# Running all sixteen retention pairs ahead of the gated unit's first sweep

## The chip, the core and the metric

The kernel is one program on one core of a Trainium2 chip. Five engines work side by side, each through its own queue in order: TensorE (PE in the profile, with its weight loads as PEld), VectorE (DVE), ScalarE (ACT), GpSimd (POOL) and the queue that issues most DMAs (SP). The metric is the device time of one execution in microseconds, and lower is better.

## The reference

Three layers follow each other on 2304 tokens (4 batches of 576) of 512 features:

```python
# 1. retention: 8 heads of 64, decay gamma per head
scores = scale * np.matmul(q, k.transpose(0, 1, 3, 2))
Dmat = np.where(rel >= 0, gamma[:, None, None] ** rel[None, :, :], 0.0)
x = np.matmul(scores * Dmat[None], v)            # -> (2304, 512)
# 2. gated unit behind an RMS norm, d_ff = 1536
xn = x / np.sqrt(np.mean(x * x, axis=-1, keepdims=True) + 1e-06) * rms_g
g = xn @ w_gate
x = g * (1.0 / (1.0 + np.exp(-g))) * (xn @ w_val) @ w_out
# 3. eight experts (512 -> 1024 -> 512), mixed by 8 rounds of Sinkhorn on exp(x @ w_gate)
for e in range(8):
    out += P[:, e:e + 1] * (np.maximum(x @ w1[e], 0.0) @ w2[e])
```

## The kernel before, in words

The program is recorded in the order in which the Python code runs, and each engine executes its instructions in that order; buffers of the tile pools and the waits on them are the only other ties. So the order of work around the change is an order written out by hand.

**Retention.** The 32 heads are worked in 16 pairs (4 batches of 4 pairs; pair `i` is written `sc_i`, `am_i`, `o_i`). A pair has 576 tokens in four blocks of 128 and a tail of 64. `scores(i)` makes k·q of each block and head on PE (tile `sc`, one PSUM buffer per head), and DVE masks it (`am`). `states(i)` makes k·v of each block (`u`), which ACT and DVE turn into running states (`block_states`). `outputs(i)` makes `o` and `ot` from `am`, the states and the tail `mt`; DVE writes them to `acc`, ACT squares them, POOL adds the squares of a batch's pairs. The pass of the loop for pair `i` issues `scores(i + 1)`, `states(i + 1)` and then `outputs(i)`. Since `sc` has one buffer per head, `scores(i + 1)` waits until DVE has made `am_i`.

**Norm.** `norm(b)` is a generator that the loop steps: sums over the features on PE (`ss`), the root on DVE and POOL, a spread over partitions by PE (`dg`, `rb`, `rbt`, then `y`), and for each 128 features a product on DVE (L404), a high part on ACT (`xhi`, L405) and a low part on DVE or POOL (`xlo`, L408 and L410).

**Gated unit.** `gated_block(s, t0, n, ...)` works `n` tokens with 256 of the 1536 inner features; a sweep `s` is all tokens, and there are six sweeps. A product of full precision is three fp32r matmuls (L174 to L176: high·high, high·low, low·high). A block has 48 of them for the gate and value (`gv`) and 24 for the way back (`x`). Behind each pair of `gv` DVE multiplies (L202), ACT takes the high part (`ghi`, L203) and DVE the low part (`glo`, L204), which the `x` matmuls read. In the first sweep ACT writes `x` to `acc` (L223), in the later ones DVE adds it (L225).

**Weights.** They arrive as 64-bit floats. `step_weights()` brings up to two pieces of 128x512 one step forward: a start (L122 on POOL, L123 and L124 on DVE), the sign step (L126 on DVE, L127 on ACT), a product (POOL), the high part into a slot (ACT) and the low part (L144 on DVE). There are seven slots (`wslots`, `NW = 7`); six pieces make a sweep.

**The first sweep in the retention.** Before, the first sweep runs over eight blocks of 288 tokens (`FIRST_BLOCKS`) as a stream (`dense`) out of which `fill()` takes a quarter of a block's `gv`, or half of its `x`, at a time, from pair 7 on, between `scores`/`states` and `outputs`. Earlier passes have `keep_busy(3)` at two places: three bf16 matmuls of 128x512 on a pad, whose result nobody reads. What is left of the stream runs behind the last pair, with the first block of the second sweep begun inside it (`second_sweep`). Sweeps 1 to 5 then run in a plain loop over five blocks of 512 or 384 tokens (`BLOCKS`).

Of the kernel before, what the change touches and what calls it, by code (L numbers as in the profile page):

```python
# [18 lines left out]
NP = H // 2  # L19
# [11 lines left out]
FIRST_BLOCKS = [(b * S + h * (S // 2), S // 2) for b in range(B) for h in range(2)]  # L31
# [6 lines left out]
N_DENSE = 15  # L38
# [12 lines left out]
def retention_glu_experts(ctx: ExitStack, tc: tile.TileContext, a, out):  # L51
# [43 lines left out]
    slots = [[(wslots[:, i, 0, :], wslots[:, i, 1, :]) for i in range(NW)], []]  # L95
    raw_slots = list(range(NRAW))
# [82 lines left out]
    def gated_block(s, t0, n, last, pmm, pac, hp, tp, together, w):  # L179
# [27 lines left out]
        for d0 in range(0, KD, together):  # L207
            ys = [(pac[0] if type(pac) is list else pac).tile([128, 512], F32, tag="ac", name=f"x{s}_{t0}_{d0 + d}") for d in range(together)]
# [24 lines left out]
    def in_turn(blocks):  # L233

        before = ()
        for ready, block in blocks:
            while not ready():
                yield
            next(block)
            yield  # L240
            for _ in before:
                yield
            for _ in range(2 * SWEEP - 1):
                next(block)
                yield
            before = block
        for _ in before:
            yield


    early = ExitStack()
    hp0 = early.enter_context(tc.tile_pool(name="hp0", bufs=SWEEP + 1))
    tp0 = early.enter_context(tc.tile_pool(name="tp0", bufs=2))
# [6 lines left out]
    pmm0 = early.enter_context(tc.tile_pool(name="pmm0", bufs=2, space=PSUM, side="right"))  # L260
    pac0 = early.enter_context(tc.tile_pool(name="pac0", bufs=2, space=PSUM, side="right"))
# [5 lines left out]
    mhalf = tabs.tile([128, NC + 1], F32, name="mhalf")  # L267
    block_states = [tabs.tile([128, NC, 2 * D], F32, name=f"block_states{i}") for i in range(2)]
# [3 lines left out]
    def load_pair(i):  # L272
        if i >= B * NP:
            return
        b, pr = divmod(i, NP)
        t = {}
        for n in ("kT", "qT", "ks", "vs"):
            t[n] = ld.tile([128, a[n].shape[-1]], F32, tag=n, name=f"{n}{i}", bufs=2 if n[0] == "k" else 3)
            nc.sync.dma_start(t[n], a[n][b, pr])
        loaded[i] = t  # L280
# [34 lines left out]
    def states(i):  # L315
# [12 lines left out]
        for h, hs in enumerate(heads):  # L328
            nc.scalar.mul(st[hs, :, hs], u[hs, :NC, :], g_step[hs, pr:pr + 1])
# [7 lines left out]
    def outputs(i):  # L337
# [4 lines left out]
        o = psa.tile([128, NC, C], F32, tag="o", name=f"o{i}")  # L342
        ot = pac0.tile([128, 512], F32, tag="ac", name=f"ot{i}")[:, :TAIL]
# [25 lines left out]
    normed = set()  # L369

    def norm(b):

        sq = squares.pop(b)
        ss = pac0.tile([128, 512], F32, tag="ac", name=f"ss{b}")[:, :NC + 1]
# [3 lines left out]
        v = sp.tile([128, NC + 1], F32, tag="rv", name=f"rv{b}")  # L378
        r = sp.tile([128, NC + 1], F32, tag="ry", name=f"ry{b}")
        t = sp.tile([128, NC + 1], F32, tag="rt", name=f"rt{b}")  # L380
# [8 lines left out]
        dg = sp.tile([128, (NC + 1) * C], F32, tag="dg", name=f"dg{b}", bufs=1)  # L389
# [23 lines left out]
    def first_group():  # L413
        for t0, n in FIRST_BLOCKS:
            block = gated_block(0, t0, n, t0 + n == NT, pmm0, pac0, hp0, tp0, 2, S // 2)
            yield (lambda b=t0 // S: b in normed), block

    dense = in_turn(first_group())

    norms = []  # L420

    def fill():
        next(dense, None)
        step_weights(load=False)

    def norm_step(n=1):
        for _ in range(n):
            if norms and next(norms[0], True):
                norms.pop(0)

    idle = pad[:, :128]
    idle_ps = pmm0.tile([128, 512], F32, tag="mm", name="idle_ps")
# [19 lines left out]
    load_pair(1)  # L452
# [6 lines left out]
    states(0)  # L459
    for i in range(B * NP):  # L460
        b, pr = divmod(i, NP)
        load_pair(i + 2)
# [5 lines left out]
        if i <= NP + 2:  # L468
            keep_busy(3)
        if i == NP + 1:  # L470
            norm_step()
        scores(i + 1)
        states(i + 1)
        if i <= NP + 1:
            keep_busy(3)
            outputs(i)
            for _ in range(3 if i < NP else 1):
                step_weights(load=False)
            if i >= NP:
# [35 lines left out]
    for _ in dense:  # L515
        pass
# [795 lines left out]
```

## Time and profile before

| | |
|---|---|
| time of three runs | 2068.27 us median (2065.36 to 2070.55) |
| profiled execution | 2068.53 us, span 2066.6 us from the first to the last instruction |
| mean granted TensorE clock | 0.992 of full speed |
| PE busy | 2035.1 us, 98% of the span |
| DVE busy | 1482.2 us, 72% |
| ACT, POOL busy | 862.9 us, 842.9 us |
| DMA | 211 GB/s in the mean |

The span is counted from the first instruction to the last; the execution's own time holds 1.9 us more. The granted clock is given as a share of 2.4 GHz, and 0.50 is the lower level of 1.2 GHz. A busy PE need not be a useful one: the filler matmuls count, and a matmul at the lower clock counts twice as long.

### The profile page before, as it was taken

How to read it: one execution, taken by the hardware profiler on the slowest of the kernel's cores; microseconds unless marked ns; L12 is line 12 of the kernel's file. 1: busy time of each engine (PE TensorE's matmuls, PEld its weight loads, DVE VectorE, ACT ScalarE, POOL GpSimd, SP SyncE). 2: the span in 40 equal slices, each digit the busy share in tenths (PEclk: the TensorE clock that was granted, in tenths of full speed). 3: DMA queues.
4: the chain of work that ended last, by engine and by line, in shares of the span. 5: the costliest groups of instructions: out<-in, count | busy, mean ns of one | idle time of the engine just before them, and what ended most of it. 6: DMA issues, size and time to landing. Idle time of an engine off the chain costs nothing.

```text
span 2066.6 us, 30376 instructions
## 1 busy us (share of the span) xinstructions
PE 2035.1 (98%) x11526; PEld 1883.8 (91%) x11526; DVE 1482.2 (72%) x2324; ACT 862.9 (42%) x1655; POOL 842.9 (41%) x746
## 2 busy tenths in 40 slices
PE   8999999999999999999999999999999999999998
PEld 5688788899788989999998999999999999999998
DVE  6764775653468887777776777777788677777777
ACT  3443331221254454444444544444445544444443
POOL 4411442310024454544561545444455454544443
PEclk8899999999999999999999999999999999999999
DMA  7420221100028888888878767676766676767673
GB/s 233 156 90 1 69 75 41 62 29 3 0 96 306 296 297 299 309 300 306 306 285 329 262 252 275 244 268 247 280 246 260 251 273 252 260 251 281 241 282 138
DMA packets 112690, 436.58 MB, mean 211 GB/s; under 512 B 12297, under 2 KB 30473, under 8 KB 96161
## 3 DMA queue, kind: packets, MB, share of 16 engines
q1 hardware_dynamic: 110048, 432.72, 57.4%
q8 instruction: 90, 1.47, 0.3%
q10 hardware_dynamic: 2496, 1.94, 0.3%
q14 instruction: 56, 0.45, 0.1%
HBM read 312.40 MB, written 122.21 MB: 210 GB/s over the span
## 4 chain that ended last, share of the span: by engine, by line
PE 89%; DVE 6%; ACT 2%; issue 1%; POOL 1%; DMA 1%; ACTq 0%; SPq 0%; DVEq 0%; POOLq 0%
PE pz L775 9%; PE py L775 9%; PE px L775 9%; PE qx L1006 6%; PE qy L1006 6%; PE qz L1006 6%; PE gv L174 5%; PE gv L175 4%; PE gv L176 4%; PE y L175 4%; PE y L176 4%; PE y L174 4%; PE qz L775 3%; PE x L174 2%; PE x L175 2%; PE x L176 2%
## 5 line engine op out<-in xcount | busy, mean ns | idle before, releaser
L1183 POOL TENSOR_TENSOR acc<-z,a_block 128x384 f32<-128x384 f32 x63 | 64.0, 1016 | 446.5 <-DVE z L1177 446.5
L775 PE MATMUL py<-sx,w1s 128*128 128x384 f32 x1152 | 233.0, 336 | 2.8 <-ACT py L1099 2.5
L775 PEld LDWEIGHTS py<-sx,w1s 128*128 128x128 f32 x1152 | 203.5, 188 | 7.2 <-ACT py L1099 4.3
L775 PE MATMUL px<-xhi,w1s 128*128 128x384 f32 x640 | 188.5, 335 | 0.0
L996 ACT CAST xhi<-acc 128x384 fp32r<-128x384 f32 x316 | 156.0, 514 | 69.6 <-POOL acc L1183 35.4
L1000 DVE TENSOR_TENSOR xlo<-acc,xhi 128x384 fp32r<-128x384 f32 x191 | 177.5, 956 | 1.8 <-ACT xhi L996 1.8
L1000 POOL TENSOR_TENSOR xlo<-acc,xhi 128x384 fp32r<-128x384 f32 x125 | 145.4, 1163 | 32.2 <-ACT xhi L996 32.2
L1014 DVE TENSOR_TENSOR acc<-acc,qz 128x384 f32<-128x384 f32 x246 | 134.9, 548 | 26.0 <-PE qz L1006 26.0
L577 POOL TENSOR_TENSOR t<-rw 128x256 f32<-128x256 f32 x32 | 43.0, 1343 | 234.6 <-issue 126.9
L122 POOL TENSOR_SCALAR cv<-raw 128x512 f32<-128x512 f32 x36 | 63.1, 1757 | 182.6 <-DVE wslots L144 91.6
L175 PE MATMUL gv<-xlo,wslots 128*128 128x512 f32 (+2 forms) x368 | 127.4, 346 | 3.0 <-DVE xlo L408 1.7
L174 PE MATMUL gv<-xhi,wslots 128*128 128x512 f32 (+2 forms) x368 | 128.5, 349 | 0.4 <-ACT xhi L405 0.4
L176 PE MATMUL gv<-xhi,wslots 128*128 128x512 f32 (+2 forms) x368 | 126.9, 345 | 0.0
L202 DVE TENSOR_TENSOR t<-t,gv 128x512 f32<-128x512 f32 (+2 forms) x66 | 38.8, 589 | 115.8 <-PE gv L176 115.7
L775 PEld LDWEIGHTS px<-xhi,w1s 128*128 128x128 f32 x640 | 117.9, 188 | 0.3
L1014 DVE TENSOR_TENSOR acc<-acc,qx 128x384 f32<-128x384 f32 x123 | 67.4, 548 | 70.1 <-PE qx L1006 70.1
L775 PE MATMUL pz<-xhi,w1s 128*128 128x384 f32 x384 | 113.8, 337 | 3.2 <-DVE z L930 2.3
L775 PE MATMUL pz<-sx,w1s 128*128 128x384 f32 x576 | 115.6, 335 | 0.0
L775 PE MATMUL px<-xlo,w1s 128*128 128x384 f32 x320 | 106.9, 334 | 0.0
L820 DVE SCALAR_TENSOR_TENSOR acc<-y,prob,acc 128x512 f32<-128x512 f32 x144 | 101.4, 742 | 6.1 <-PE y L176 6.1
L176 PE MATMUL y<-xlo,xhi 128*128 128x512 f32 x264 | 103.9, 393 | 0.0
L175 PE MATMUL y<-xlo,xhi 128*128 128x512 f32 x264 | 103.7, 393 | 0.0
(379 smaller groups left out, 6037.4 us busy)
## 6 DMA issues: line engine op xcount, KB each, us to landing
w1s<-w_kept SPq DMA_DIRECT2D x64, 1792.0 KB, 7.1
w_kept<-w1s SPq DMA_DIRECT2D x32, 1792.0 KB, 6.6
rw<-in_w_dram SPq DMA_DIRECT2D x64, 512.0 KB, 5.5
w_kept<-xlo SPq DMA_DIRECT2D x64, 512.0 KB, 3.7
w2s<-w_kept SPq DMA_DIRECT2D x32, 1024.0 KB, 6.9
w_extra<-w_kept SPq DMA_DIRECT2D x32, 768.0 KB, 7.6
w_kept<-xlo SPq DMA_DIRECT2D x44, 384.0 KB, 4.1
w2c<-w_kept SPq DMA_DIRECT2D x32, 512.0 KB, 7.7
```

Source lines behind the costliest of these rows:

```text
L122: nc.gpsimd.tensor_scalar(sign, high_f, -least, None, ALU.is_le)
L174: nc.tensor.matmul(ps, lhsT=lh, rhs=rh, start=start, stop=False)
L175: nc.tensor.matmul(ps, lhsT=lh, rhs=rl, start=False, stop=False)
L176: nc.tensor.matmul(ps, lhsT=ll, rhs=rh, start=False, stop=stop)
L577: nc.gpsimd.tensor_sub(t[:, 0, :], w[:, 3, :], w[:, 0, :])
L775: nc.tensor.matmul(ps, lhsT=l, rhs=r[:, k, :], start=start and k == 0 and i == 0, stop=k == 1 and i == 2, skip_group_check=True,)
L820: nc.vector.scalar_tensor_tensor(o, y_2, pe, o, ALU.mult, ALU.add)
L996: nc.scalar.copy(hi, x)
L1000: (engine or nc.vector).tensor_sub(lo, x, f32(hi))
L1006: nc.tensor.matmul(ps, lhsT=l, rhs=r, start=start and i == 0, stop=i == 2, skip_group_check=True)
L1014: nc.vector.tensor_add(dst, dst, ps)
L1183: nc.gpsimd.tensor_add(sums[0], z[:, 0, :], h_blocks[0])
```

## The change

All sixteen pairs now run before any block of the gated unit, with fillers only in the first two passes. The first sweep becomes the first turn of the loop over `BLOCKS`, with blocks of 512 and 384 tokens. The norm is cut into `norm_sums` (sums and root) and `norm` (spread and products), of which the loop takes one step a pass, two in odd passes from 7 on, and the first sweep takes the rest: one or two steps behind each step of a block. The products for `dg` move from DVE to ACT. `block_states` keeps the two heads side by side in 64 columns, so that each state matmul becomes two of 64x64 and ACT scales both heads at once. The loads of a pair are split: `kT` and `ks` of pair `i + 3` behind `states(i + 1)`, `qT` and `vs` of pair `i + 2` at the head of the pass. One step of the weights is taken in each pass, and three more slots (`w_more`) open behind the retention.

```diff
-FIRST_BLOCKS = [(b * S + h * (S // 2), S // 2) for b in range(B) for h in range(2)]
...
+    pac = ctx.enter_context(tc.tile_pool(name="pac", bufs=4, space=PSUM, side="right"))
...
-        for h, hs in enumerate(heads):
-            nc.scalar.mul(st[hs, :, hs], u[hs, :NC, :], g_step[hs, pr:pr + 1])
+        nc.scalar.mul(st, u[:, :NC, :], g_step[:, pr:pr + 1])
...
-                nc.tensor.matmul(dst, lhsT=st[:, c - 1, :], rhs=qt[:, c * C:min(S, c * C + C)], start=True, stop=False)
+                for hs in heads:
+                    cs = slice(c * C, min(S, c * C + C))
+                    nc.tensor.matmul(dst[hs, :], lhsT=st[hs, c - 1, :], rhs=qt[hs, cs], start=True, stop=False)
...
+    def norm(b):
+        r = rstd.pop(b)
+        dg = nrm.tile([128, (NC + 1) * C], F32, tag="dg", name=f"dg{b}")
         dg = dg.rearrange("p (c i) -> p c i", i=C)
         for c in range(NC + 1):
-            nc.vector.tensor_scalar(dg[:, c, :], ident, r[:, c:c + 1], None, ALU.mult)
+            nc.scalar.mul(dg[:, c, :], ident, r[:, c:c + 1])
...
+    def norm_step():
+        if sums_due:
+            if next(sums_due[0], True):
+                sums_due.pop(0)
+            return
+        b = len(normed)
+        if b in norms or b in rstd:
+            if b not in norms:
+                norms[b] = norm(b)
+            next(norms[b], None)
...
     for i in range(B * NP):
         b, pr = divmod(i, NP)
-        load_pair(i + 2)
+        load_pair(i + 2, "qT", "vs")
         load_weights()
...
-        if i <= NP + 2:
+        if i < 2:
             keep_busy(3)
...
         scores(i + 1)
         states(i + 1)
-        if i <= NP + 1:
+        load_pair(i + 3, "kT", "ks")
+        if i < 2:
             keep_busy(3)
...
+        step_weights(load=False)
+        outputs(i)
+        norm_step()
+        if i > NP + 2 and i % 2:
             norm_step()
         if pr == NP - 1:
-            norms.append(norm(b))
...
+            sums_due.append(norm_sums(b))
...
+    w_more = wmore.tile([128, 3, 2, 512], F32R, name="w_more")
+    slots[0] += [(w_more[:, i, 0, :], w_more[:, i, 1, :]) for i in range(3)]
...
-    for s in range(1, NSWEEP):
+    for s in range(NSWEEP):
...
+            while not s and (t0 + n - 1) // S not in normed:
+                norm_step()
...
+                next(block)
+                if not s:
+                    for _ in range(1 + i % 2):
+                        norm_step()
```

In the changed program line 174 is 176, 202 is 204, 303 is 282, 309 is 288, 404 is 389 and 408 is 393.

On PE, between `outputs(9)` and `scores(11)`, the program before has half of the `x` of the first block (these rows are the first of twelve of the kind):

```order
L350 MATMUL ot_1122<-mt_969,vs_834 64x64 x2
L174 MATMUL x_0_2_1147<-ghi_0_0_883,wslots 128x288
L175 MATMUL x_0_2_1147<-glo_0_0_884,wslots 128x288
L176 MATMUL x_0_2_1147<-ghi_0_0_883,wslots 128x288
L174 MATMUL x_0_3_1148<-ghi_0_0_883,wslots 128x288
L175 MATMUL x_0_3_1148<-glo_0_0_884,wslots 128x288
```

At the like place, between `outputs(10)` and `scores(12)`, the changed program has nothing:

```order
L330 MATMUL o_1020<-am_10_904,vs_815 64x128
L330 MATMUL o_1020<-am_10_905,vs_815 64x128
L328 MATMUL ot_1021<-qT_813,block_states_119 64x64 x2
L330 MATMUL ot_1021<-mt_926,vs_815 64x64 x2
L282 MATMUL sc_12_1057<-qT_976,kT_932 128x128
L282 MATMUL sc_12_1058<-qT_976,kT_932 128x128
```

The matmuls that stood between the pairs are gone from there, so that PE goes from pair to pair.

On DVE, pass 9 is now the fullest of the retention; from the masks of pair 10 to those of pair 11 it reads (`cv` and `raw` are the weights, `ry` and `y` the norm of batches 1 and 0):

```order
L288 SCALAR_TENSOR_TENSOR am_10_905<-sc_10_903,g_in,causal 128x512
L308 SCALAR_TENSOR_TENSOR mt_926<-u_901,g_tail,causal_t 128x64
L310 SCALAR_TENSOR_TENSOR block_states_119<-block_states_119,g_step 128x64 x3
L146 TENSOR_TENSOR wslots<-cv_623,wslots 128x512
L128 SCALAR_TENSOR_TENSOR cv_854<-raw_661,cv_854 128x512
L125 TENSOR_SCALAR cv_939<-raw_738 128x512
L126 SCALAR_TENSOR_TENSOR cv_939<-raw_738,cv_939 128x512
L337 TENSOR_TENSOR acc<-o_943,g_out 128x512
L341 TENSOR_TENSOR acc<-ot_944,g_out 128x64
L366 TENSOR_TENSOR rt_892<-ry_891 128x5
```

Behind these come two small steps of the root, L389 and L393 for batch 0, and then `am_11`. Weights and norm now stand together in one pass of the retention.

In the first block of the first sweep, DVE has before, between the low part of one half and the product of the next, one instruction of the norm (here the fifth of the eight blocks):

```order
L202 TENSOR_TENSOR t_1152_0_1793<-t_1152_0_1793,gv_1152_0_1_1849 128x288
L204 TENSOR_TENSOR glo_1152_0_1863<-t_1152_0_1793,ghi_1152_0_1862 128x288
L404 SCALAR_TENSOR_TENSOR acc<-acc,rms_g,y_1886 128x576
L202 TENSOR_TENSOR t_1152_1_1880<-t_1152_1_1880,gv_1152_1_1_1891 128x288
L204 TENSOR_TENSOR glo_1152_1_1905<-t_1152_1_1880,ghi_1152_1_1904 128x288
```

In the changed program, the second block (tokens 512 to 1023) has between the same two:

```order
L206 TENSOR_TENSOR glo_512_0_1665<-t_512_0_1641,ghi_512_0_1664 128x512
L389 SCALAR_TENSOR_TENSOR acc<-acc,rms_g,y_1623 128x576
L393 TENSOR_TENSOR xlo<-acc,xhi 128x576
L389 SCALAR_TENSOR_TENSOR acc<-acc,rms_g,y_1623 128x576
L146 TENSOR_TENSOR w_more<-cv_1533,w_more 128x512
L128 SCALAR_TENSOR_TENSOR cv_1647<-raw_1537,cv_1647 128x512
L125 TENSOR_SCALAR cv_1678<-raw_1560 128x512
L126 SCALAR_TENSOR_TENSOR cv_1678<-raw_1560,cv_1678 128x512
L389 SCALAR_TENSOR_TENSOR acc<-acc,rms_g,y_1623 128x576
L393 TENSOR_TENSOR xlo<-acc,xhi 128x576
L128 SCALAR_TENSOR_TENSOR cv_1678<-raw_1560,cv_1678 128x512
L204 TENSOR_TENSOR t_512_1_1697<-t_512_1_1697,gv_512_1_1_1707 128x512
```

The norm of batch 2 and the conversion of two pieces now stand between the two halves of the block. In the first block there are two L389, one L393 and the same four of the weights, in the third block four L389 and two L393.

## Rows read from the trace of the kernel before

**Rows 1.** Busy time by stretch: us, PE, PEld, DVE, ACT, POOL, clock, DMA share, GB/s.
```profile
0.00:90.00 90.00, 80.31 (x650) 52.26 (x651) 67.35 (x124) 36.37 (x71) 38.16 (x32) 0.85 0.60 196
...
240.00:310.00 70.00, 69.80 (x341) 61.54 (x339) 54.53 (x76) 22.00 (x40) 30.88 (x20) 1.00 0.24 76
```

**Rows 2.** Timeline of PE at the full clock: start us, us, instruction.
```profile
19.80 1.16 PE L303 MATMUL sc<-qT,kT 64*128 64x128 f32 x16
...
21.77 0.82 PE L437 MATMUL idle_ps<-pad 128*128 128x512 bf16 x3
22.52 0.44 PE L350 MATMUL o<-am,vs 128*64 128x128 f32 x4
...
25.88 0.82 PE L437 MATMUL idle_ps<-pad 128*128 128x512 bf16 x3
```

**Rows 3.** Timeline of PE around a fall of the clock.
```profile
35.60 2.73 PE L303 MATMUL sc<-qT,kT 64*128 64x128 f32 x16 [2.07 <-DVE am L309]
...
39.73 1.46 PE L437 MATMUL idle_ps<-pad 128*128 128x512 bf16 x3
41.12 0.70 PE L350 MATMUL o<-am,vs 128*64 128x128 f32 x4
41.74 0.71 PE L348 MATMUL o<-qT,block_states 128*128 128x128 f32 x2
```

**Rows 4.** Busy time by stretch, with the granted clock behind POOL.
```profile
35.50:42.20 6.70, 6.60 (x45) 4.54 (x45) 3.19 (x9) 1.79 (x3) 3.24 (x3) 0.50 0.94 319
...
73.00:86.50 13.50, 11.11 (x64) 9.20 (x64) 11.56 (x20) 6.33 (x13) 5.45 (x4) 0.50 0.30 103
...
228.00:235.00 7.00, 3.29 (x13) 2.10 (x12) 6.15 (x8) 2.40 (x4) 3.71 (x3) 1.00 0.24 75
```

**Rows 5.** Timeline of PE: the matmuls of a norm.
```profile
52.98 1.15 PE L377 MATMUL ss<-ones,sq 128*128 128x1 f32 x10
...
62.64 1.13 PE L396 MATMUL rb<-dg,ones 128*128 128x512 f32 x2 [0.31 <-DVE dg L392]
```

**Rows 6.** DVE's groups from 90 to 240 us: count, busy us, mean ns, idle before.
```profile
L404 DVE SCALAR_TENSOR_TENSOR acc<-acc,rms_g,y 128x576 f32<-128x576 f32 x12 | 10.7, 909 | 4.9 <-ACT y L400 4.9
L309 DVE SCALAR_TENSOR_TENSOR am<-sc,g_in,causal 128x512 f32<-128x512 f32 x14 | 9.8, 742 | 4.1 <-PE sc L303 4.1
...
L408 DVE TENSOR_TENSOR xlo<-acc,xhi 128x576 fp32r<-128x576 f32 x6 | 6.7, 1124 | 0.0
L357 DVE TENSOR_TENSOR acc<-o,g_out 128x512 f32<-128x512 f32 x9 | 6.2, 691 | 14.2 <-PE o L350 14.2
L124 DVE SCALAR_TENSOR_TENSOR cv<-raw,cv 128x512 int32<-128x512 int32 x5 | 5.1, 1016 | 0.2
L123 DVE TENSOR_SCALAR cv<-raw 128x512 int32<-128x512 int32 x5 | 4.0, 791 | 0.1
L126 DVE SCALAR_TENSOR_TENSOR cv<-raw,cv 128x512 f32<-128x512 f32 x4 | 3.8, 954 | 0.0
L144 DVE TENSOR_TENSOR wslots<-cv,wslots 128x512 fp32r<-128x512 f32 x5 | 3.4, 688 | 0.2
...
L361 DVE TENSOR_TENSOR acc<-ot,g_out 128x64 f32<-128x64 f32 x9 | 2.0, 224 | 0.0
L330 DVE SCALAR_TENSOR_TENSOR mt<-u,g_tail,causal_t 128x64 f32<-128x64 f32 x7 | 2.0, 281 | 1.8 <-ACT block_states L329 1.8
L204 DVE TENSOR_TENSOR glo<-t,ghi 128x512 fp32r<-128x512 f32 x2 | 1.4, 692 | 1.4 <-ACT ghi L203 1.4
```

**Rows 7.** Timeline of PE: the first matmul of the third sweep.
```profile
295.90 0.39 PE L174 MATMUL gv<-xhi,sx 128*128 128x512 f32 x1
```

**Rows 8.** Timeline of DVE: first sums of the first block of sweeps 2 to 4.
```profile
237.46 1.87 DVE L225 TENSOR_TENSOR acc<-acc,x 128x512 f32<-128x512 f32 x3
...
310.42 0.69 DVE L225 TENSOR_TENSOR acc<-acc,x 128x512 f32<-128x512 f32 x1 [1.26 <-PE x L176]
...
384.51 2.05 DVE L225 TENSOR_TENSOR acc<-acc,x 128x512 f32<-128x512 f32 x3 [1.26 <-PE x L176]
```

More of the change, by code (lines that the diff above doesn't have):

```diff
@@ L207, in gated_block @@
         for d0 in range(0, KD, together):
-            ys = [(pac[0] if type(pac) is list else pac).tile([128, 512], F32, tag="ac", name=f"x{s}_{t0}_{d0 + d}") for d in range(together)]
+            ys = [pac.tile([128, 512], F32, tag="ac", name=f"x{s}_{t0}_{d0 + d}") for d in range(together)]
             for m in range(SWEEP):
@@ L231, in gated_block @@
             yield
[L233 to L253, printed above, removed]
     retention = ExitStack()
@@ L266, in retention_glu_experts, with load_pair @@
     g_out = tabs.tile([128, NP, C], F32, name="g_out")
-    mhalf = tabs.tile([128, NC + 1], F32, name="mhalf")
-    block_states = [tabs.tile([128, NC, 2 * D], F32, name=f"block_states{i}") for i in range(2)]
+    mhalf = nrm.tile([128, NC + 1], F32, name="mhalf")
+    block_states = [tabs.tile([128, NC, D], F32, name=f"block_states{i}") for i in range(2)]
     heads = [slice(h * D, (h + 1) * D) for h in range(2)]
     loaded, staged, squares = {}, {}, {}
-    def load_pair(i):
+    def load_pair(i, *names):
         if i >= B * NP:
@@ L276, in load_pair @@
         t = {}
-        for n in ("kT", "qT", "ks", "vs"):
+        for n in names:
             t[n] = ld.tile([128, a[n].shape[-1]], F32, tag=n, name=f"{n}{i}", bufs=2 if n[0] == "k" else 3)
             nc.sync.dma_start(t[n], a[n][b, pr])
-        loaded[i] = t
+        loaded.setdefault(i, {}).update(t)
     def scale_keys(i):
@@ L367, in outputs, with norm_sums @@
         squares[b] = sq
-    normed = set()
-    def norm(b):
+    normed, rstd = set(), {}
+    def norm_sums(b):
         sq = squares.pop(b)
-        ss = pac0.tile([128, 512], F32, tag="ac", name=f"ss{b}")[:, :NC + 1]
+        ss = pac.tile([128, 512], F32, tag="ac", name=f"ss{b}")[:, :NC + 1]
         for c in range(NC + 1):
@@ L411, in norm @@
         normed.add(b)
[L413 to L429, printed above, removed]
+    sums_due = []
+    def norm_step():
[8 more added lines that the diff above has]
+            next(norms[b], None)
+    norms = {}
     idle = pad[:, :128]
-    idle_ps = pmm0.tile([128, 512], F32, tag="mm", name="idle_ps")
+    idle_ps = psa.tile([128, 512], F32, name="idle_ps")
     def keep_busy(n):
@@ L506, in retention_glu_experts @@
     pmm = glu_ps.enter_context(tc.tile_pool(name="pmm", bufs=4, space=PSUM))
-    hp = glu.enter_context(tc.tile_pool(name="hp", bufs=SWEEP + 1, side="right"))
-    tp = glu.enter_context(tc.tile_pool(name="tp", bufs=3, side="right"))
-    sums = []
-    second_sweep = gated_block(1, *BLOCKS[0], False, pmm, sums, hp, tp, KD, 512)
-    for _ in range(N_DENSE):
-        next(dense)
-        step_weights()
-    next(second_sweep)
-    for _ in dense:
-        pass
-    early.close()
-    pac = ctx.enter_context(tc.tile_pool(name="pac", bufs=4, space=PSUM, side="right"))
-    sums.append(pac)
     xpool = ctx.enter_context(tc.tile_pool(name="xpool", bufs=1))
@@ L666, in retention_glu_experts @@
             block = gated_block(s, t0, n, last, pmm, pac, hp, tp, 1 if last_sweep and last else KD, 512)
-            if s == 1 and not j:
-                block = second_sweep
+            while not s and (t0 + n - 1) // S not in normed:
+                norm_step()
             for i in range(2 * SWEEP + 1):
@@ L671, in retention_glu_experts @@
                     break
-                if i or block is not second_sweep:
-                    next(block)
+                next(block)
+                if not s:
+                    for _ in range(1 + i % 2):
+                        norm_step()
                 if i != 2 * SWEEP - 1:
```

58 lines of the change are left out of this document (17 added, 41 removed).

## The prediction

> **What bounds the kernel now.** I read the busy time by stretch first. From 240 us on PE has no idle time (69.80 of 70 us), with DVE at 54.5 of 70 beside it; in the first 90 us PE is busy for 80 of 90, but at a mean clock of 0.85 and with fillers among its work [rows 1]. So the place to look at is the stretch up to the first sums of the second sweep, which DVE begins at 237.46 us [rows 8]. I call this the **mark**. Behind it both programs do the same work with PE full, so a shift of the mark is the shift of the end. The three more weight slots can give nothing there, since there is no idle time to give.
>
> Second, the timeline of PE in the retention. At the full clock scores and states of a pair take 1.97 us (19.80 to 21.77) and its outputs 3.36 (22.52 to 25.88), 5.33 together; a group of fillers takes 0.75 [rows 2]. Where DVE is late with a mask, PE waits ahead of the next scores: 2.07 us before 35.60. Then the clock is at 0.50 for 6.7 us [rows 3, 4]. At that level scores and states take 4.13 us (35.60 to 39.73), and a step of the outputs takes 0.70 for 0.44, about 1.5 times as long [rows 2, 3]. A pair is then about 4.1 + 1.5 x 3.36 = 9.2 us, 3.8 more than at the full clock. The longest stretch at 0.50 is 13.5 us [rows 4]. Yet a wait of over 2 us at 228 to 231 us, in dense matmuls (PE is busy for 3.29 of 7 us there), leaves the clock at 1.00 [rows 4].
>
> **The change, part by part.** I build up the new mark.
>
> *The retention, PE alone.* Passes 0 and 1 keep their fillers, so pair 1's outputs end at 25.88 as before [rows 2]. Then come 13 passes of 5.33 us and the last outputs of 3.36: 72.7. Three sums of a norm at 1.15 and two spreads at 1.13 add 5.7 [rows 5]. PE would be done at 104.3. The split of each state matmul in two of half height and width has no row; the nearest are a step of two half-width matmuls and a step of one whole, 0.70 and 0.71 at the lower clock [rows 3], so I take no difference. The one scaling on ACT for two lies beside it.
>
> *DVE in the retention.* A pair needs two masks (1.48), the tail (0.28), three steps of the states, which are now 64 wide (I take the tail's 0.28 each), and two products (0.91): 3.5 us [rows 6]. A start of a weight piece is 1.81, its sign step 0.95, its low part 0.69; a norm product is 0.91 and a low part 1.12 [rows 6]. Over most passes that is less than PE's 5.33. Pass 5 (low part, sign step, start) comes to 7.0, pass 9 (the same, one norm product, one low part) to 9.0, pass 11 to 6.7, pass 13 to 7.0. Scores need only the mask of the pair before, which is ready 5.33 - 1.16 - 1.48 = 2.7 us early when PE sets the pace; this slack takes pass 5's 1.6. Pass 9 exceeds by 3.7 and leaves a wait of 1.0; passes 11 and 13 leave about 1 each. So 3 us, between 0 (all in the slack) and some 9 (if DVE is slowed as much as in the first 90 us, where it is busy for 67 of 90 [rows 1]); I take 4. PE waits ahead of `scores`, and `outputs` behind it.
>
> *Loads.* A pair loads 1.15 MB. The first 90 us move 196 GB/s at a share of 0.60, so some 325 at most [rows 1], and a pair's loads need 3.5 us of its 5.33. Their throughput is hidden; but `qT` and `vs` of pair `i + 2` are issued only when the outputs of `i - 1` have left their buffers, one pair ahead of use. I take 2 us in all, between 0 and 1 us for each of 14 pairs.
>
> *The clock.* The fillers that stood between the late pairs are gone, and the dense matmuls too. Where PE waits a microsecond or more per pass, the clock may fall as at 35 us. I take two stretches at 0.50, as long as the two of rows 4: 20 us, 2.2 pairs of 9.2, so 2.2 x 3.8 = 8.4. The bounds are 0, and ten pairs or 38 us. The Trainium skill ("TensorE: Matmul & The Clock Gate", section "A second HAM failure mode: psum-queue depth-cycling") says that PE pausing briefly but often between groups of matmuls can make the clock swing between its levels, so that throughput suffers though each matmul at the full level is as fast as ever. That speaks against taking the fillers out; by it the term of 8.4 would go towards its upper bound, which is the second rival below.
>
> The retention thus ends at 104.3 + 4 + 2 + 8.4 = 118.7.
>
> *The first sweep.* The next sweep's rows give its cost: blocks of the same size, 384.51 - 310.42 = 74.1 us for a sweep, and 310.42 - 295.90 = 14.5 from a sweep's first matmul to its first sums [rows 7, 8]. Before, eight blocks of 288 did the same. On PE one more sum (1.15) and two spreads (2.26) come in: 3.4.
>
> *DVE in the first sweep.* Now look at what stands between the halves of a block in DVE's queue. From the first half's product to the `x` matmuls of the second half PE has 36 of a block's 72 matmuls; a block of 512 is 74.1 x 512 / 2304 = 16.5 us, so PE has 8.2 us of work. DVE has product, high part (ACT) and low part, three steps of about 0.69 (2.1), twice, and between them: in the first block two norm products, a low part and for the weights a low part, two sign steps and a start, 7.4; in the second 9.4, in the third 5.0 [rows 6]. That is 11.5, 13.5 and 9.1 against 8.2: PE waits for `glo` by 3.3, 5.3 and 0.9, together 9.5. The last two blocks have no norm left. The lower bound is 0, since in the second sweep DVE is busy for 78% with PE full [rows 1]; the upper is 15, if each wait of DVE on ACT or POOL adds. I take 9.5. One fall of the clock behind these waits, 6.7 us at half speed, adds 3.4 (0 by the wait at 228 us [rows 4], 7 if twice).
>
> *Covered.* The five scalings of `dg` on ACT (36.4 us busy of 90 [rows 1]) stand a pass ahead of their spread; without that cover PE would wait some 1.5 us per norm. The three more slots keep DVE from waiting with pieces 7 to 9.
>
> **Sum.** 118.7 + 74.1 + 14.5 + 3.4 + 9.5 + 3.4 = 223.6 for the mark, 13.9 earlier than 237.46. The profiled execution took 2068.53, so 2054.6; the median is 0.26 lower than it, so I predict 2054.4.
>
> **The rivals.**
>
> *Smooth.* The clock never falls and DVE's lumps reach PE nowhere in the sweep: 8.4, 9.5 and 3.4 go, mark 202.3, time 2033. For it: the wait at 228 us left the clock alone. Against it: the fall at 35 us, and DVE's queue is in order, so the lumps can't be passed.
>
> *The clock stays low.* This is the other side. From pass 5 on, where DVE's surplus begins, PE runs at 0.50 until the sweep: 10.6 pairs x 3.8 = 40 in place of 8.4, less the 4 of DVE's waits, which the slower PE hides. The mark comes to 251, the time to 2082. It decides at 2.2 + 13.9 / 3.8 = 5.9 low pairs, where nothing is gained. For it: no stretch of pairs without fillers or dense work has been seen to hold the clock. Against it: between 35.5 and 42.2 us it came back within two pairs [rows 4].
>
> *A draw.* Four to seven low pairs, or loads that cost 1 us per pair: the mark within 6 us of 237, the time 2062 to 2074.
>
> **How the numbers follow.** I give my forecast (2042 to 2062) 0.42, smooth 0.15, a draw 0.25, the clock low or a like loss 0.18. A difference of 0.3% is 6 us, about what runs between 2065 and 2071 can tell. Faster is the forecast and smooth, 0.57; same is the draw, 0.25; slower 0.18. The range reaches from 2037, which leaves out most of smooth's better half, to 2076, which leaves out the worse cases of the low clock. Around the forecast alone it is 2042 to 2062.
>
> **What would show it.** The last outputs of the retention should end near 119 us, and the mark be near 224. Pairs at the full clock should be 5.3 us apart where DVE is light, and PE's waits ahead of scores should fall in passes 9, 11 and 13, with DVE's `am` named. The clock should be at 0.50 for some 20 us between 25 and 119. In the first sweep PE should wait for `glo` in the first two blocks, 3 and 5 us, not in the last two. I am wrong if the clock is low for over half of the retention, if loads are what PE waits for, or if something behind the mark moves.

## The result

The changed kernel took 2050.6 us in the median of four runs (2047.0 to 2052.8), beside 2068.05 for the kernel before: a ratio of 0.9914, with a 95% interval of 0.9895 to 0.9933. That is 17.5 us or 0.86% faster. The forecast was 2054.4, so direction and size held. The way there did not hold everywhere, and one edit that I had costed at nothing was worth 8 us, on the wrong side.

The profiled execution is the fastest of the four (2047.01 us, span 2045.2). First its stretches and the four places at the lower clock (columns as in [rows 1]):

```profile
0.00:90.00 90.00, 83.25 (x1022) 55.52 (x1022) 72.53 (x152) 38.85 (x81) 35.77 (x31) 0.91 0.77 251
240.00:310.00 70.00, 69.81 (x341) 61.56 (x340) 52.62 (x75) 19.40 (x36) 27.41 (x18) 1.00 0.22 66
73.00:86.70 13.70, 12.42 (x110) 9.14 (x112) 13.05 (x22) 5.45 (x11) 7.56 (x5) 0.50 0.57 182
103.80:110.60 6.80, 6.80 (x41) 4.04 (x38) 2.66 (x5) 3.43 (x7) 3.59 (x3) 0.50 0.28 80
127.70:131.10 3.40, 3.29 (x8) 2.62 (x9) 0.72 (x2) 1.98 (x5) 0.00 (x0) 0.50 0.26 104
151.60:155.00 3.40, 3.38 (x7) 2.44 (x8) 1.36 (x2) 2.14 (x7) 0.13 (x1) 0.50 0.37 140
```

Against [rows 1] the first 90 us hold over half as many matmuls again (1022 for 650; the split of the state matmuls alone makes some 104 of them), at a clock of 0.91 for 0.85. From 240 us on PE is as full as before (69.81 of 70 us). The marks stand in DVE's timeline, at the first sums of the second and third sweep, and answer to [rows 8]:

```profile
214.44 0.69 DVE L227 TENSOR_TENSOR acc<-acc,x 128x512 f32<-128x512 f32 x1 [1.27 <-PE x L178]
...
289.18 1.37 DVE L227 TENSOR_TENSOR acc<-acc,x 128x512 f32<-128x512 f32 x2 [1.26 <-PE x L178]
```

The mark came 23.0 us earlier (237.46 to 214.44; forecast 13.9), and the second sweep took 74.7 where it took 73.0 before. From the mark to the end it was 1829.1 us before and 1830.8 after. So the whole gain lies ahead of the mark. The 1.7 us behind it are hardly a new cost: in the kernel before, DVE came late to the mark, with no wait ahead of its row in [rows 8], and the sums of the second block followed 14.5 us later, for 16.3 now.

A pair at the full clock, in PE's timeline, answers to [rows 2] (L282 is the old L303, L328 the old L348, L330 the old L350):

```profile
23.40 1.16 PE L282 MATMUL sc<-qT,kT 64*128 64x128 f32 x16
...
25.59 0.44 PE L328 MATMUL o<-qT,block_states 64*64 64x128 f32 x4
25.95 0.44 PE L330 MATMUL o<-am,vs 128*64 128x128 f32 x4
...
28.17 1.16 PE L282 MATMUL sc<-qT,kT 64*128 64x128 f32 x16
```

Pair 1's outputs end at 23.40, and pairs are 4.77 us apart. I had 25.88 and 5.33.

What PE waits for between 18 and 230 us (total, times, longest), and in its timeline the longest wait for a mask and the wait for `acc`, up to the first sweep:

```profile
PE x L176 <- ACT ghi L205: 6.9, 2, 4.4
PE sc L282 <- DVE am L288: 3.5, 2, 3.4
PE o L330 <- DVE acc L337: 1.9, 1, 1.9
PE x L177 <- DVE glo L206: 0.4, 2, 0.2
```

```profile
74.28 2.73 PE L282 MATMUL sc<-qT,kT 64*128 64x128 f32 x16 [3.37 <-DVE am L288]
...
83.19 2.08 PE L282 MATMUL sc<-qT,kT 64*128 64x128 f32 x16
...
101.31 0.43 PE L381 MATMUL rbt<-dg,ones 64*128 64x64 f32 x2
103.60 0.54 PE L330 MATMUL o<-am,vs 128*64 128x128 f32 x4 [1.85 <-DVE acc L337]
...
108.44 0.79 PE L176 MATMUL gv<-xhi,wslots 128*128 128x512 f32 x1
```

The retention ends at 108.5 (forecast 118.7), the sweep up to the mark takes 105.9 (forecast 104.9).

### The profile page after: what moved, and what is told of

Its sections match the earlier page's. It is cut to its first block, busy times and chain, and to the rows that moved or that the text cites. A ratio compares the mean times of both kernels' runs of the same rounds, so it can differ in the third digit from the quotient of the medians.

```text
span 2045.2 us, 30056 instructions
## 1 busy us (share of the span) xinstructions
PE 2011.9 (98%) x11402; PEld 1860.0 (91%) x11402; DVE 1470.7 (72%) x2292; ACT 855.3 (42%) x1635; POOL 840.3 (41%) x744
## 4 chain that ended last, share of the span: by engine, by line
PE 88%; DVE 8%; ACT 2%; issue 1%; DMA 1%; POOL 1%; ACTq 0%; SPq 0%; DVEq 0%; POOLq 0%
PE py L726 9%; PE pz L726 9%; PE px L726 9%; PE qx L957 6%; PE qy L957 6%; PE qz L957 6%; PE gv L176 4%; PE gv L177 4%; PE gv L178 4%; PE y L177 4%; PE y L178 4%; PE y L176 4%; PE qz L726 3%; PE x L177 2%; PE x L178 2%; PE x L176 2%
## 5 line engine op out<-in xcount | busy, mean ns | idle before, releaser
L124 POOL TENSOR_SCALAR cv<-raw 128x512 f32<-128x512 f32 x36 | 63.4, 1765 | 179.9 <-DVE wslots L146 56.7
L204 DVE TENSOR_TENSOR t<-t,gv 128x512 f32<-128x512 f32 (+1 forms) x60 | 37.9, 632 | 125.8 <-PE gv L178 125.8
L726 PE MATMUL pz<-sx,w1s 128*128 128x384 f32 x576 | 115.7, 335 | 0.0
L178 PE MATMUL y<-xlo,xhi 128*128 128x512 f32 x264 | 104.0, 394 | 0.0
L177 PE MATMUL y<-xlo,xhi 128*128 128x512 f32 x264 | 103.7, 393 | 0.0
L983 ACT COPY qz<-qy 128x384 f32<-128x384 f32 x127 | 58.8, 463 | 107.0 <-PE qy L957 99.4
L176 PE MATMUL y<-xlo,xhi 128*128 128x512 f32 x264 | 102.9, 390 | 0.0
L726 PEld LDWEIGHTS pz<-sx,w1s 128*128 128x128 f32 x576 | 101.2, 188 | 0.4
```

The source lines that it names most:

```text
L124: nc.gpsimd.tensor_scalar(sign, high_f, -least, None, ALU.is_le)
L176: nc.tensor.matmul(ps, lhsT=lh, rhs=rh, start=start, stop=False)
L177: nc.tensor.matmul(ps, lhsT=lh, rhs=rl, start=False, stop=False)
L178: nc.tensor.matmul(ps, lhsT=ll, rhs=rh, start=False, stop=stop)
L726: nc.tensor.matmul(ps, lhsT=l, rhs=r[:, k, :], start=start and k == 0 and i == 0, stop=k == 1 and i == 2, skip_group_check=True,)
L983: nc.scalar.copy(z, y)
```

## The experiments

All runs against the same kernel before, whose medians in the four sessions were 2067.4 to 2068.6. "Retention" is the end of the last outputs, "sweep 1" from there to the mark, "sweep 2" from the mark to the next sweep's first sums, all in the profiled execution.

Two cautions. The runs of e1, e2, e4, e7, e10, e11 and e15 do not overlap those of the changed kernel (2047.0 to 2052.8); those of e3, e5, e6, e8 and e12 do, so that their medians alone show no difference. And only one execution of each kernel is profiled, while the clock falls at other places from one execution to the next. The changed kernel, e6 and e15 issue the same instructions up to the new fillers at 66.8 us; in these stretches the clock was at 0.50 from 8.2 to 11.6 us in the first, from 60.8 to 64.2 in the second and from 12.7 to 16.1 in the third.

| kernel | median (range), us | ratio, 95% | retention | sweep 1 | sweep 2 |
|---|---|---|---|---|---|
| changed | 2050.6 (2047.0–2052.8) | 0.9895–0.9933 | 108.5 | 105.9 | 74.7 |
| e1 whole states | 2056.8 (2053.7–2059.3) | 0.9922–0.9957 | 115.7 | 105.6 | 74.8 |
| e2 fillers in all passes | 2061.2 (2059.1–2062.9) | 0.9946–0.9976 | 119.8 | 105.7 | 74.9 |
| e3 no weights in norm blocks | 2048.1 (2046.1–2049.1) | 0.9879–0.9912 | 110.5 | 99.6 | 79.5 |
| e4 blocks of 288 in sweep 1 | 2062.1 (2059.4–2066.2) | 0.9956–0.9977 | 108.3 | 119.9 | 74.8 |
| e5 no weights in pass 9 | 2050.0 (2049.3–2054.1) | 0.9908–0.9933 | 110.1 | 107.4 | 74.8 |
| e6 fillers in two waits | 2047.0 (2045.5–2053.1) | 0.9893–0.9920 | 106.0 | 105.9 | 74.7 |
| e7 seven slots | 2042.6 (2040.0–2042.9) | 0.9863–0.9890 | 108.3 | 101.7 | 73.0 |
| e8 = e3 + e6 | 2046.0 (2042.9–2048.3) | 0.9882–0.9909 | 111.3 | 99.4 | 79.5 |
| e10 slots join later | 2056.1 (2053.4–2058.8) | 0.9932–0.9957 | 109.9 | 105.6 | 84.2 |
| e11 = e7 + e6 | 2041.1 (2039.6–2044.5) | 0.9859–0.9887 | 106.1 | 101.5 | 73.0 |
| e12 spread in its own bank | 2050.2 (2046.9–2053.1) | 0.9905–0.9932 | 105.7 | 108.2 | 74.8 |
| e15 weight steps elsewhere | 2038.2 (2036.5–2041.4) | 0.9836–0.9869 | 107.9 | 94.9 | 75.7 |

### One part undone: states, fillers, block size

**e1** puts the states back to full width, as before.

```diff
-        nc.scalar.mul(st, u[:, :NC, :], g_step[:, pr:pr + 1])
+        for h, hs in enumerate(heads):
+            nc.scalar.mul(st[hs, :, hs], u[hs, :NC, :], g_step[hs, pr:pr + 1])
...
-                for hs in heads:
-                    cs = slice(c * C, min(S, c * C + C))
-                    nc.tensor.matmul(dst[hs, :], lhsT=st[hs, c - 1, :], rhs=qt[hs, cs], start=True, stop=False)
+                nc.tensor.matmul(dst, lhsT=st[:, c - 1, :], rhs=qt[:, c * C:min(S, c * C + C)], start=True, stop=False)
```

> The changed kernel with the states of both heads in 128 columns again, and one state matmul of 128x128 in place of two of 64x64. If the split is what brings a pair from 5.33 to 4.77 us, pairs at the full clock are some 0.5 us further apart again, the retention's last outputs end at 114 to 116 us in place of 108.5, and the time is 5 to 7 us longer. If the shorter pair comes from the missing fillers and waits alone, pairs stay at 4.8 us and the time within 2 us.

It came 6.2 us above the changed kernel. PE's timeline in e1:

```profile
25.63 1.16 PE L282 MATMUL sc<-qT,kT 64*128 64x128 f32 x16
...
28.61 0.49 PE L327 MATMUL o<-qT,block_states 128*128 128x128 f32 x2
...
30.81 1.16 PE L282 MATMUL sc<-qT,kT 64*128 64x128 f32 x16
```

A pair takes 5.18 us: the split is worth 5.18 - 4.77 = 0.41 a pair. The other 0.15 of what I had (5.33) I put down to the breaks beside the fillers, which no run shows by itself.

**e2** takes away the condition `if i < 2` from both `keep_busy(3)`.

> The changed kernel with three fillers at both places in every pass. If the clock costs less than the fillers: 26 groups of 0.75 us are 20 us more work on PE, less the 5 us in which it waits for DVE and some 9 us for 20 us at the lower clock; the clock stays at 1.00 from 12 us to the end of the retention and the time is about 6 us longer. If the missing fillers are a loss, as the rule on brief pauses would have it, the time is 3 us or more shorter.

10.6 us above the changed kernel. The clock is at 1.00 from 16 us to the end of the retention, as hoped, but between 18 and 120 us the 90 filler matmuls take 24.5 us of PE, and the retention ends 11.3 us later. To let the clock fall is cheaper than to hold it up in this way.

**e4** gives the first sweep the old blocks.

```diff
-        for j, (t0, n) in enumerate(BLOCKS):
+        blocks = BLOCKS if s else FIRST_BLOCKS
+        for j, (t0, n) in enumerate(blocks):
```

> The changed kernel with its first sweep in eight blocks of 288 tokens. If the block size is part of the gain, the first sweep takes some 8 to 9 us more on PE and the time is 6 to 9 us longer; if PE's waits for DVE set the sweep, and eight blocks give DVE more room, the time is within 3 us.

11.5 us above. PE waits 14.8 us for `ghi`, in four blocks (the longest 6.8), for 6.9 in two: a smaller block gives PE less to do while DVE works off its queue.

### The waits of the retention

**e5** leaves the weight steps of pass 9 out.

```diff
+        if i != 9:
-        step_weights(load=False)
+            step_weights(load=False)
```

> Pass 9 leaves its three steps of the weight piece out (every later step is one pass late, the sweeps catch up). The theory is that DVE's surplus of pass 9 makes PE wait 3.37 us ahead of the next scores at 70.92 to 74.28 us, and that the 13.7 us at half clock from 73 us on follow from this wait. Then the wait shrinks below 1 us, the clock stays at 1.00 there, the retention's last outputs end some 3 + 6 us earlier (near 99 to 101 us), and the whole is 5 to 8 us below the changed kernel's 2050.6. Rival: the surplus only moves to passes 10 and 11, a wait of 2 us or more stands there and the clock falls there: within 2 us of the changed kernel.

The rival held in the time, not in the wait of 2 us that it foretold. The waits for the mask are now five of at most 1.0 us, but the clock falls all the same, at 80.9 us. PE's waits (18 to 230 us) and the stretch (columns as above):

```profile
...
PE sc L282 <- DVE am L288: 2.2, 5, 1.0
PE o L330 <- DVE acc L337: 2.1, 1, 2.1
...
```

```profile
80.90:94.50 13.60, 13.60 (x118) 9.80 (x118) 11.79 (x23) 4.98 (x11) 6.82 (x5) 0.50 0.41 143
```

**e6** puts fillers at the two long waits: seven before the outputs that waited for `acc`, and twelve before the scores of pair 11, which is a pair ahead of the longest wait (it stood before the scores of pair 12).

```diff
-        if i < 2:
-            keep_busy(3)
+        if i < 2 or i == 10:
+            keep_busy(3 if i < 2 else 12)
...
         step_weights(load=False)
+        if i == 15:
+            keep_busy(7)
```

> 12 fillers ahead of the scores that waited 3.37 us at 70.92 us, and 7 ahead of the outputs that waited 1.85 us at 101.75 us: PE is busy in the two places and waits as long as before. If it is PE's idle time that takes the clock down, the falls at 73 us (13.7 us long) and 104 us (6.8 us) go, about 20 us at half speed, so some 8 us back: 2042 to 2045. Rival: the falls come from something else in these stretches (the mix of matmuls, the work before them): they stay and the time is that of the changed kernel or 1 to 2 us above.

The median is 3.6 us lower, under half of what the theory gave, and the runs overlap (2045.5 to 2053.1). The long waits went. In this execution the two long falls went too, and two of 3.4 us came at 60.8 and 88.1, the first of them before any new filler had run. In the place of the longest:

```profile
73.00:86.70 13.70, 12.43 (x174) 8.68 (x170) 13.49 (x23) 7.08 (x15) 7.51 (x5) 1.00 0.81 263
```

The clock is full, and DVE is now busy for 13.49 of 13.70 us. With PE at its full speed DVE leaves next to no room here, and the retention ends only 2.5 us earlier, though behind 18 us it has 6.8 us at the lower clock in place of 18.4. That the fillers hold the clock up is not shown: e8, e11 and e15 have the same retention, and behind the fillers the clock was low for 10.2 us in e8, 3.4 in e11 and 10.2 in e15. In e15:

```profile
77.60:87.70 10.10, 10.10 (x98) 6.99 (x96) 9.96 (x16) 4.36 (x8) 5.87 (x4) 0.50 0.50 166
```

With the fillers the retention ends at 106.0, 111.3, 106.1 and 107.9 us (e6, e8, e11, e15), without them at 108.5, 110.5, 108.3, 108.3 and 109.9 (changed, e3, e4, e7, e10). By these ends they gain a microsecond or two, if anything.

**e12** writes `rb` of the first two norms to the fillers' bank.

```diff
-        rb = pac.tile([128, NC * C], F32, tag="ac", name=f"rb{b}")
+        rb = (psa if b < 2 else pac).tile([128, NC * C], F32, tag="idle_ps" if b < 2 else "ac", name=f"rb{b}")
```

> The spread of the first two norms writes the PSUM bank of the fillers instead of one of the four that outputs, sums and spreads share. Theory: the wait of 1.85 us ahead of the outputs at 101.75 us is a wait for a bank (the outputs of pair 15 need the bank that DVE's product of pair 14 still reads), so it goes (below 0.4 us), the fall of the clock at 103.8 us (6.8 us long, 3.4 lost) goes with it: 3 to 6 us below the changed kernel, 2045 to 2048. Rival: the outputs wait there for DVE in any case, on the mask or on the scaled keys behind the same product: within 2 us of 2050.6, and the wait stands under another name.

The wait for the bank is gone, so that cause of the wait is shown. The gain did not come (the runs overlap those of the changed kernel). PE's waits from 18 to 230 us, without a line for `o`:

```profile
PE x L176 <- ACT ghi L205: 6.4, 2, 4.4
PE sc L282 <- DVE am L288: 3.7, 3, 3.4
PE ss L357 <- POOL sq L346: 1.7, 1, 1.7
...
```

The retention ends at 105.7, but then the last batch's sums wait 1.7 us for POOL's squares, and the fall comes behind that, at 113.4. Sweep 1 is 2.3 us longer.

### The weight steps in the first sweep

**e3** leaves the weight steps out of the first three blocks of the first sweep.

```diff
-                if i != 2 * SWEEP - 1:
+                if i != 2 * SWEEP - 1 and (s or j > 2):
```

> The changed kernel with no step of the weights in the first three blocks of the first sweep, where the norm's rest is. If PE waits for the high parts because weights and norm stand together in DVE's queue, its two waits of 2.5 and 4.4 us and the falls of the clock behind them go, the first sums of the second sweep move from 214.4 to about 205 us, and the time is 7 to 10 us shorter. If the norm alone makes the waits, or the weights then come late in the second sweep, the time stays within 2 us, and PE waits for the slots behind 180 us.

2.5 us in place of 7 to 10. Sweep 1 gained 6.3, and sweep 2 gave 4.8 of it back: from 210 to 300 us PE waits 2.1 us for `ghi` and 1.5 for `glo`, where the changed kernel waits for nothing. **e8** puts e3 and e6 together.

> The fillers at the two waits of the retention (as in the run with fillers at the waits) and no weight steps in the first three blocks of the first sweep (which alone came to 2048.1). If the two are independent: 2.5 us below the run with fillers at the waits alone, so 2040 to 2043. If the falls of the clock don't depend on PE's idle time: 2047 to 2049.

2046.0, where the sum of the two would be 2044.5; its runs (2042.9 to 2048.3) do not tell these apart. Sweep 2 is at 79.5 again.

**e7** leaves out the three more slots.

```diff
-    wmore = glu.enter_context(tc.tile_pool(name="wmore", bufs=1))
-    w_more = wmore.tile([128, 3, 2, 512], F32R, name="w_more")
-    slots[0] += [(w_more[:, i, 0, :], w_more[:, i, 1, :]) for i in range(3)]
```

> The three more weight slots are left out, the rest stands. The prediction held that they give next to nothing behind the mark, since PE is full there. Theory: within 3 us of the changed kernel (two waits of the kernel before for slots, of a microsecond or two, may come back at the second sweep, and the first sweep converts fewer pieces, so its waits of 2.5 and 4.4 us shrink). Rival: they are needed, since a sweep that runs out of pieces stops PE: 5 us or more above the changed kernel.

Faster by 8.0 us, which neither theory had. A weight step that finds no free slot records nothing, so the number of slots decides how much DVE converts ahead of need. DVE, ACT and POOL on the tiles `cv`, first in the changed kernel, then with seven slots:

```profile
108.00:142.00 34.00, 7.35 (x11) 3.13 (x5) 7.64 (x5) 0.91 0.10 31
142.00:158.00 16.00, 4.68 (x5) 1.25 (x2) 4.41 (x3) 0.89 0.23 68
```

```profile
108.00:142.00 34.00, 2.48 (x4) 0.63 (x1) 3.35 (x2) 0.97 0.05 16
142.00:158.00 16.00, 0.00 (x0) 0.00 (x0) 0.00 (x0) 1.00 0.00 1
```

Ten slots put 12.03 - 2.48 = 9.6 us more on DVE in the very blocks that hold the norms. With seven PE hardly waits there: the `x` matmuls of the first two blocks take 5.6 and 6.4 us, for 10.4 and 12.0. What comes instead, in the second sweep's first block and still ahead of the mark, is smaller (PE's waits, 18 to 230 us), and no fall of the clock follows it:

```profile
...
PE x L178 <- DVE wslots L146: 2.4, 1, 2.4
...
PE x L176 <- ACT wslots L144: 1.3, 1, 1.3
...
```

**e11** is e7 with the fillers of e6.

> Seven slots and the fillers at the two waits of the retention together. Alone they came to 2042.6 and 2047.0, 8.0 and 3.6 below the changed kernel. They act in different stretches (the first sweep, the retention), so if they add up: 2038 to 2041. If the fall of the clock that the fillers take away comes back in another place of the retention: 2042 to 2044.

2041.1, within the spread of e7: nothing that the fillers add can be told from it.

**e10** lets the three slots join at the first sweep's fourth block.

```diff
-    slots[0] += [(w_more[:, i, 0, :], w_more[:, i, 1, :]) for i in range(3)]
...
+            if not s and j == 3:
+                slots[0] += [(w_more[:, i, 0, :], w_more[:, i, 1, :]) for i in range(3)]
```

> The three more slots join the list of free ones only at the fourth block of the first sweep, when the norms are done. Theory after the run with seven slots: the slots cost time because DVE converts three more pieces in the blocks in which it also has the norms. Then the x matmuls of the first two blocks take 5.6 and 6.4 us as with seven slots (10.4 and 12.0 in the changed kernel), and since the pieces are there before the second sweep, its first block doesn't wait either (10.2 us of x matmuls with seven slots, 5.6 in the changed kernel): 4 us or so below the run with seven slots' 2042.6, that is 2037 to 2040. Rival: the pieces come too late either way, and the second sweep waits as with seven slots: 2042 to 2044. A second rival: it was the slots' place in memory or their number that cost the time: 2048 to 2052.

The first half held (5.6 and 6.5 us of `x` matmuls in the first two blocks), the total did not: 2056.1, since the fourth and fifth blocks wait 2.6 and 1.5 us, the clock is low for 6.8 us behind the first of these waits, and sweep 2 takes 84.2. DVE's queue in a block of sweep 2:

```profile
241.62 0.69 DVE L206 TENSOR_TENSOR glo<-t,ghi 128x512 fp32r<-128x512 f32 x1 [0.69 <-ACT ghi L205]
242.23 0.68 DVE L146 TENSOR_TENSOR sx<-cv,sx 128x512 fp32r<-128x512 f32 x1
242.95 0.43 DVE L125 TENSOR_SCALAR cv<-raw 128x512 int32<-128x512 int32 x1
243.41 1.01 DVE L126 SCALAR_TENSOR_TENSOR cv<-raw,cv 128x512 int32<-128x512 int32 x1
...
246.43 0.69 DVE L126 SCALAR_TENSOR_TENSOR cv<-raw,cv 128x512 int32<-128x512 int32 x1
247.04 0.68 DVE L204 TENSOR_TENSOR t<-t,gv 128x512 f32<-128x512 f32 x1
```

Seven weight instructions stand between the first half's low part and the second half's product. In the same block of the changed kernel there are three (240.29 to 242.50), and DVE then waits 1.25 us for PE. Here PE waits for DVE. A restart at another moment shifts which step of a piece falls into which part of the block, and the pattern repeats from block to block.

**e15** tests that place itself, with ten slots and the fillers of e6.

```diff
-                if i != 2 * SWEEP - 1:
+                for _ in range((1, 0, 0, 1, 2)[i]):
                     step_weights()
```

> Ten slots and the fillers at the two waits of the retention (2047.0 before this edit); the four weight steps of a block no longer stand after its parts 0, 1, 2 and 4, but after 0, 3 and twice after 4, so that none lies in DVE's queue between the low part of the first half and the product of the second. Theory: what makes PE wait in the first sweep is not the slots but these steps in this place (3.6 us of them beside 3.9 us of norm work in the first block). Then the x matmuls of the first two blocks, 10.5 and 12.4 us long before the edit, come down to 8 or less, the falls of the clock behind the waits go, and the later sweeps stay at 5.6 per block: 4 to 8 us gained, 2039 to 2043. Rival: two steps in a row behind a block put DVE late for the next block's first half, or for its sums, and PE waits there in each block of all sweeps: 2050 or more.

2038.2, 8.8 us below e6 and the lowest median of all (its runs overlap those of e7 and e11). DVE in the first block, first in the changed kernel, then in e15:

```profile
117.89 0.94 DVE L206 TENSOR_TENSOR glo<-t,ghi 128x512 fp32r<-128x512 f32 x1 [0.69 <-ACT ghi L205]
...
119.95 0.68 DVE L146 TENSOR_TENSOR w_more<-cv,w_more 128x512 fp32r<-128x512 f32 x1
120.56 0.68 DVE L128 SCALAR_TENSOR_TENSOR cv<-raw,cv 128x512 f32<-128x512 f32 x1
...
122.66 1.85 DVE L389 SCALAR_TENSOR_TENSOR acc<-acc,rms_g,y 128x576 f32<-128x576 f32 x1
...
125.70 0.68 DVE L204 TENSOR_TENSOR t<-t,gv 128x512 f32<-128x512 f32 x1
```

```profile
116.89 0.94 DVE L206 TENSOR_TENSOR glo<-t,ghi 128x512 fp32r<-128x512 f32 x1 [0.69 <-ACT ghi L205]
...
118.22 1.54 DVE L389 SCALAR_TENSOR_TENSOR acc<-acc,rms_g,y 128x576 f32<-128x576 f32 x2
119.78 0.76 DVE L393 TENSOR_TENSOR xlo<-acc,xhi 128x576 fp32r<-128x576 f32 x1
120.96 0.69 DVE L204 TENSOR_TENSOR t<-t,gv 128x512 f32<-128x512 f32 x1 [0.42 <-PE gv L178]
```

From low part to product it was 7.8 us and is now 4.1, the last 0.42 of it a wait for PE. The `x` matmuls of the first two blocks take 5.6 and 6.4, the clock is at 1.00 from 87.8 us until long after the mark, and sweep 1 is 11.0 us shorter than in e6. The rival's loss is there but small: sweep 2 takes 1 us more than in e6.

## Why the prediction was right, and where it was not

**The bound and the mark.** Right. PE is full behind the mark in both kernels, and the gain stands ahead of it. But the mark came at 214.4 for 223.6, which is 9.1 us of error, while the time is only 3.8 below the forecast: in part because the profiled execution is 3.6 below the median. The nearness of the number is partly luck.

**The retention, PE alone (104.3).** Too high by about 9.6. "The split of each state matmul ... I take no difference" was the mis-sized term: with the fillers' breaks gone as well, a pair takes 4.77 for 5.33, which is 13 x 0.56 + 0.5 for the last outputs = 7.8 us. e1 shows 0.41 of the 0.56 to be the split. I had read its price from a step at the lower clock [rows 3], where the halves and the whole look alike. The start came 2.5 earlier: 0.8 are two split outputs, 0.5 the first states, which PE begins at 8.47 for 9.02, and 1.1 the second pair's scores and states, which run mostly at the full clock (10.91 to 13.27) where before they ran at the lower (11.46 to 14.93). The norm's matmuls cost some 0.7 more.

**DVE's waits (4).** They were 5.4. The kind was right for pass 9 (3.4 us for a forecast of 1.0). The mis-sized pair carries over here: by the forecast's own working a pair of 4.77 us gives a surplus of 9.0 - 4.77 = 4.2 and a slack of 4.77 - 1.16 - 1.48 = 2.1, so an estimated wait of 2.1; and the low part took 1.97 us for 1.12, beside POOL (last section). Passes 11 and 13 brought nothing, and 1.85 us went to a wait that I had not seen: spread and outputs share four PSUM banks (e12). In e5, with pass 9 lightened, five passes wait: the surplus belongs to several passes, not to pass 9 alone.

**Loads (2).** No wait for them: 0.

**The clock (8.4, from 20 us low).** It was low for 13.7 + 6.8 us. At that level a pair took 8.91 us (74.28 to 83.19) for 4.77, which is 1.87 times as long and not twice; the next, half at that level, took 6.34, and the last outputs 4.91 (103.60 to 108.51) for 2.90. So 4.1 + 1.6 + 2.0 = 7.7 us were lost. The size is right, but by luck in part: other executions of the same retention had less or more (see below). It did not stay low, as the second rival had it. The rule of the Trainium skill ("TensorE: Matmul & The Clock Gate", section "A second HAM failure mode: psum-queue depth-cycling"), by which brief pauses between groups make the clock swing, agrees in kind: it fell at 73.1 us and came back at 86.7, fell at 103.8 and came back at 110.6.

Together 118.7 - 7.8 - 2.5 + 0.7 + 1.4 - 2 - 0.7 = 107.8, for 108.5 measured. Of the 0.7 left some 0.5 stand in pair 10, whose scores PE begins in two parts (65.42 and 66.08).

**The first sweep (74.1 + 14.5 + 3.4, waits 9.5, clock 3.4).** The mechanism was right: PE waits for the second half's high part behind DVE's queue. The `x` matmuls of the first three blocks take 10.4, 12.0 and 6.4 us, where 5.6 is a block without a wait; in the first two the clock is low for 3.4 us each, which costs 1.6 (matmuls begin 0.43 us apart there, 0.23 otherwise). That leaves 3.2, 4.8 and 0.8 us of waiting (forecast 3.3, 5.3 and 0.9), 8.8 together, and none of size in the last two blocks. The clock is low for 2.1 + 3.4 + 3.4 us behind 108.5, which is 4.1 lost. The rest is 93.0 for 92.0.

**The three slots.** This step failed: "the three more weight slots can give nothing there", and "the three more slots keep DVE from waiting with pieces 7 to 9". I looked at what the slots give behind the mark, and did not ask what they let DVE start ahead of it. They cost 8.0 us (e7). I had counted the weight steps between the halves in my 9.5 us, and taken them as given. e15 shows that not the slots but the steps' place is the price. The low rival (*smooth*) put the mark at 202.3; e15 reaches 202.8, but by other terms: its retention ends at 107.9 with 10.2 us at the lower clock, where *smooth* has 110.3 and none, and its sweep takes 94.9 for 92.0.

**Open.** When the clock falls, and for how long, is not settled. In the first sweep it was low for 3.4 us after a wait of 4.4, in e7 not at all after the waits of 2.4 and 1.3 us ahead of the mark, and in e5 it fell where no wait was longer than about 1 us. The length does not follow from the wait either: the changed kernel, e3, e4, e7 and e10 have the same retention and the same wait of 3.4 us before the scores of pair 12, and in or just behind it the clock went low for 13.7, 13.7, 3.4, 6.8 and 3.4 us. In e7 and e10:

```profile
72.80:79.50 6.70, 5.05 (x44) 4.00 (x44) 6.63 (x14) 3.44 (x8) 3.29 (x3) 0.50 0.62 204
```

```profile
77.20:80.50 3.30, 3.30 (x38) 2.56 (x34) 3.26 (x8) 1.43 (x3) 0.67 (x1) 0.50 0.39 92
```

What the new order is worth by itself, with the first sweep's matmuls between the pairs and all else as changed, no run shows. Whether e15 with seven slots would be faster still was not tried.

## What to carry to other kernels

When a buffer is added that lets an engine work ahead, ask in which queue the early work will stand, and what is behind it: an engine that is idle for a quarter of the time can still be late at one place of each block. Place background steps behind the last operation that the bounding engine waits for, not between two of them. And after moving work, time the following stretch too: e3 won in the first sweep and lost in the second, and e10 won in two blocks and lost in the later ones. Before a gain of a few microseconds is put down to the clock, look at a second execution of the same code.

## What the runs showed of the hardware

A product or low part of the norm on DVE that starts while POOL works on two tiles (L132, L346 or L393) takes until POOL is done and 0.6 us more; the changed kernel has seven cases up to 170 us. In the changed kernel the low part of a norm took 1.97 us beside POOL, and 0.74 at 124.43 us, where POOL stood idle. First DVE's row, then POOL's:

```profile
71.60 1.97 DVE L393 TENSOR_TENSOR xlo<-acc,xhi 128x576 fp32r<-128x576 f32 x1
```

```profile
71.34 1.61 POOL L346 TENSOR_TENSOR sq<-sq,sq 128x576 f32<-128x576 f32 x1 [1.71 <-issue]
...
122.59 1.31 POOL L132 TENSOR_TENSOR cv<-cv 128x512 f32<-128x512 f32 x1
```

POOL ends at 72.95 and DVE 0.62 later. The product at 122.66 is the same: 1.85 us for 0.81, and it ends 0.61 behind POOL's step at 123.90. In this block POOL's product for a weight piece (L132) thus costs the path time as well, beside the weight steps on DVE. Not every POOL instruction does this: beside L124, which reads one tile (120.79 to 122.63 us), DVE's L126 began at 122.05 and took 0.69 us. The Trainium skill says that a DVE instruction with two SBUF inputs contends with a POOL instruction that reads SBUF ("SBUF — State Buffer", section "Who interferes with whom"), and calls the ports that they share an exclusive lock. The rows shown agree; L126, which also has two inputs, was not held up beside L124.
